# Attention with a learned bias and a top-1 mixture of experts: q and k rows laid out twice by the host

## The chip, the cores and the metric

The kernel runs on one core of a Trainium2 chip. The metric is the device time of an execution in microseconds (us), of which medians are given. The engines are TensorE (PE; its weight loads are listed as PEld), VectorE (DVE), ScalarE (ACT) and GpSimd (POOL); SyncE (SP) issues most of the DMA transfers. SBUF is the on-chip memory of 128 partitions, PSUM the memory that TensorE writes its results to, HBM the device memory.

## The reference

Eight batches, eight heads, 576 tokens, head size 64, all in fp32. A small network of the log-distance of two positions gives a bias for every head, the same for all batches; the output of the attention goes through a top-1 mixture of eight experts.

```python
scores = scale * np.matmul(q, k.transpose(0, 1, 3, 2))       # B, H, S, S
x = (psi_rel / psi_i)[..., None]                             # log distances
bias = np.maximum(x @ w1 + b1, 0.0) @ w2                     # S, S, H
scores = scores + bias.transpose(2, 0, 1)[None]
attn = np.exp(scores - np.max(scores, axis=-1, keepdims=True))
attn = attn / (np.sum(attn, axis=-1, keepdims=True) + 1e-09)
x = np.matmul(attn, v)                                       # then rows of 512
...
ye = np.maximum(x[mask] @ w1[e], 0.0) @ w2[e]                # expert of the largest gate logit
out[mask] = gate_w[mask, None] * ye
```

## The kernel before

**Pairs.** The attention goes by batch and pair of heads: u = 4 b + pr, 32 pairs, each with five query tiles (four of 128 rows and one of 64). A query tile's scores for both heads go to PSUM (L253, two heads of 576 columns in halves of 288), VectorE adds the bias and takes the maximum (`less`, L275), ScalarE takes the exponential with its sum (L283), TensorE transposes (L293, L297), VectorE and ScalarE copy the transposed tiles (L304 to L312), TensorE multiplies by v (L318, L320), ScalarE copies the result (`osb`, L475), and another product with the identity turns it into token rows (`x`, L336), which VectorE scales (L351).

**Split of q and k.** TensorE multiplies in the type fp32r, so each of q and k is split into hi (rounded to fp32r) and lo (the rest). The score product contracts 128 rows: of q, hi in partitions 0 to 63 and lo in 64 to 127 (`qs`); of k, once hi in both halves (`k1`), once lo in both (`k2`). In HBM a pair's q and k lie with the first head in partitions 0 to 63 and the second in 64 to 127. `load_raw` (L211) brings them to `qn` (704 columns: 576, 64 zeros, 64 again) and `kn` (640 columns), one buffer each; `split_hi` (L217) casts on ScalarE for both heads at once; `split_lo` (L222) subtracts in place on VectorE; `move` (L236) then moves rows between partitions, by SP's queue: for q two transfers of hi and two of lo, for k four and four, each of 64 partitions.

**Opening.** The bias is made by 36 groups (`bias_group`): four `h` tiles (the first on ScalarE, L722, three on VectorE, L724; a ring of seven), eight matmuls (L729), one activation to `ob` (L731; a ring of three), and a DMA (L734) that spreads `ob` over 16 partitions eight apart of the bias tile. Pairs 0 and 1 are loaded first; ten query tiles of them (`attend`) are interleaved with the groups, with LEAD = 15 groups ahead of the first tile and RATE = 4 ahead of each that follows; pair 2 is loaded in the eighth step. The order of the instructions here is the scheduler's, by data and buffers.

**Steady pairs.** Pairs 2 to 31 run from a list of words, one string a query tile: `FULL` for pairs 2 to 29, `LAST` for 30 and 31, next to the first expert's weights. SA and SB are the two score halves, T0 to T2 transposes, p products with v, w the rest of those and the `osb` copy, x the token rows, r the routing's ranks. TensorE follows the words; VectorE and ScalarE get their order from a planner that emits whatever is due first by fixed costs. The splits and loads of the next pairs are placed by `AHEAD`, by query tile (hi, lo, load and v, with the pair that is meant and 0 for q, 1 for k). Once a batch the routing of its tokens runs on VectorE and POOL scatters its rows to HBM. After the pairs come the experts.

Of the kernel before, what the change touches and what calls it, by code (L numbers as in the profile page):

```python
# [21 lines left out]
P = 128  # L22
B, H, S, D = 8, 8, 576, 64
SH = S // 2
NPAIR = H // 2
# [7 lines left out]
QW, KW = S + 2 * 64, S + 64  # L33
# [15 lines left out]
AHEAD = [[("lo", 1, 1), ("load", 1, 0)], [("v", 1, 2)], [("load", 2, 1), ("hi", 1, 0)], [("lo", 1, 0)], [("hi", 2, 1)]]  # L49
FULL = ["SA SB T2 T0", "w SA SB T0 p p p p T2 T1 w", "SA T2 T0 SB T1 r", "SA x SB T0 p p p p T2 T1", "SA SB T0 T1 x T2"]  # L50
LAST = ["SA SB T2 T0", "w SA SB T0 p p p p T2 T1 w", "SA x T0 SB T2 T1", "SA x p p T0 SB T2 T1 p p w", "SA T0 SB p p p p w x T2 T1",
# [104 lines left out]
def attention(tc, ctx, q, kt, vm, ltab, bcst, gate, gt, cm, cmat, ival, tail0, pcst, bias, xs, plan, moe):  # L156
# [4 lines left out]
    hp_ = ctx.enter_context(tc.tile_pool(name="hi", bufs=1))  # L161
# [33 lines left out]
    def load_pair(b, pr):  # L195
        u = b * NPAIR + pr
        for x in range(2):
            load_raw(u, x)
            split_hi(u, x)
            split_lo(u, x)  # L200
            move(u, x)
        load_v(u)
# [6 lines left out]
    def load_raw(u, x):  # L209
        t = raw.tile([P, (QW, KW)[x]], F32, name=("qn", "kn")[x])  # L210
        nc.sync.dma_start(out=t, in_=(q, kt)[x][divmod(u, NPAIR)])  # L211
        raws[u, x] = [t]

    def split_hi(u, x):
        src, = raws[u, x]
        hi = hp_.tile([P, QW], F32R, name="hi")[:, :src.shape[-1]]
        nc.scalar.copy(out=hi, in_=src)  # L217
        raws[u, x].append(hi)

    def split_lo(u, x):  # L220
        src, hi = raws[u, x]
        nc.vector.tensor_tensor(out=src.bitcast(F32R), in0=src, in1=hi.bitcast(F32), op=ALU.subtract)  # L222

    def move(u, x):

        src, hi = raws.pop((u, x))
        if x:
            tiles = [kq.tile([P, 2, KW], F32R, name=n) for n in ("k1", "k2")]
            places = [[(t, h) for h in range(2)] for t in tiles]
        else:  # L230
            tiles = [kq.tile([P, 2, QW], F32R, name="qs")]
            places = [[(tiles[0], h)] for h in range(2)]
        for part, to in zip((hi.bitcast(F32), src), places):
            for t, half in to:
                for h in range(2):
                    nc.sync.dma_start(out=t[64 * half:64 * half + 64, h].bitcast(F32), in_=part[64 * h:64 * h + 64])  # L236
        loaded[u, x] = tiles
# [139 lines left out]
    def attend_units(units, words, beside):  # L377
# [139 lines left out]
        def extra(kind, u, x, *deps):  # L517
            if u >= total:
                return
            here = [(last_pe[0], 0), *deps]  # L520
            if kind == "load":
                loads[u, x] = add("any", 0, lambda: load_raw(u, x), *here, *([(subs[u - 1, x], 0.5)] if (u - 1, x) in subs else []))
            elif kind == "v":
                add("any", 0, lambda: load_v(u), *here)
            elif kind == "hi":
                splits[u, x] = add("ACT", 0.65, lambda: split_hi(u, x), *here, *([(loads[u, x], 3.0)] if (u, x) in loads else []),
                                   *([(subs["last"], 3.2)] if "last" in subs else []))
            elif kind == "lo":
                def emit():
                    split_lo(u, x)  # L530
                    move(u, x)
                subs["last"] = subs[u, x] = add("DVE", 0.77, emit, (splits[u, x], 0.8), *here)
                moved.setdefault(u, []).append((subs[u, x], 4.0))

        for k, st in enumerate(steps):
# [18 lines left out]
            beside.at(k, st, steps, add, extra, last_pe[0], ranked)  # L554
# [213 lines left out]
    class Beside:  # L768
# [12 lines left out]
        def at(self, k, st, steps, add, extra, here, ranked):  # L781
            u, qt = st["u"]["b"] * NPAIR + st["u"]["pr"], st["sc"].qt
            j = k - (len(steps) - 10)
            if j < 0:
                if k == 0:
                    extra("hi", u + 1, 1)
                for kind, v, x in AHEAD[qt]:
                    extra(kind, u + v, x)
                if j == -1:
                    extra("load", u + 2, 0)  # L790
                return
            if j == 0:
                extra("lo", u + 1, 1)
                extra("hi", u + 1, 0)
                add("DVE", 1.2, first_expert, (here, 0), (ranked[-1], 0))
            elif j == 1:
                extra("lo", u + 1, 0)
                extra("v", u + 1, 2)
# [264 lines left out]
def layout(inputs):  # L1063
# [7 lines left out]
    q = np.concatenate([q, np.zeros_like(q[..., :64]), q[..., S - 64:]], axis=-1).reshape(B, NPAIR, 2 * D, QW)  # L1071
    k = np.concatenate([k, k[..., :64]], axis=-1).reshape(B, NPAIR, 2 * D, KW)
# [57 lines left out]
```

## Time and profile before

| what | us |
|---|---|
| median of three runs | 1164.29 (1162.99 to 1167.45) |
| the profiled execution, whole | 1165.9 |
| its span in the trace | 1164.0 |
| TensorE busy | 1082.2 (93%) |
| VectorE busy | 666.7 (57%) |
| ScalarE busy | 562.4 (48%) |
| POOL busy | 169.2 (15%) |

The trace is of one execution. Busy time is a mean over stages: the opening up to about 150 us, steady pairs of 17 to 20 us up to about 685 us, then experts. A stage has to be read by itself, in the views of stretches and in the timeline; a DMA share is the mean busy share of 16 DMA engines, and can come out a little over 1, as the records of packets overlap. Of a transfer listed as DMA_DIRECT2D on SP's queue (SPq), the time is that of its issue, not of the transfer.

### The profile page before, as it was taken

Reading aid. Unit: us, or ns where it says so; the run is one execution under the profiler, and the core shown is the slowest. Engines: PE = TensorE matmul, PEld = TensorE weight load, DVE = VectorE, ACT = ScalarE, POOL = GpSimd, SP = SyncE. Lnnn points to the kernel's source line nnn. Section 1 sums busy time; section 2 is a strip of 40 time slices with the busy share of each in tenths; the row PEclk is TensorE's granted clock in tenths of the full one; section 3 lists DMA queues with packets and bytes.
Section 4 is the critical chain, followed back from the end, with each engine's and each line's share of the span. In section 5 each row is a group of like instructions: output and inputs, shape, how many; then the busy total and the mean of one; then the engine's idle time right before and its main releaser. Section 6 shows DMA issues by size and latency. Waiting matters only on the chain. (4 is left out here: it accounts for less than half of the span.)

```text
span 1164.0 us, 20696 instructions
## 1 busy us (share of the span) xinstructions
PE 1082.2 (93%) x7260; PEld 881.3 (76%) x7260; DVE 666.7 (57%) x1746; ACT 562.4 (48%) x1311; POOL 169.2 (15%) x192
## 2 busy tenths in 40 slices
PE   6599899999999999999998989999999899999894
PEld 3256687777777778787786778898888788888783
DVE  6487678787777877878778664422413232414141
ACT  5587576776767767677676631111312111313030
POOL 0000002001020010200102022500041230032320
PEclk9799999999999999999999989999999999999998
DMA  8945676767766668766777416410331600342400
GB/s 221 208 121 121 173 176 181 204 165 203 196 187 183 175 198 191 197 178 173 209 175 207 152 55 237 180 46 28 120 135 64 241 28 19 120 145 73 172 19 28
DMA packets 70084, 171.80 MB, mean 148 GB/s; under 512 B 11298, under 2 KB 11810, under 8 KB 69794
## 3 DMA queue, kind: packets, MB, share of 16 engines
q1 hardware_dynamic: 63682, 150.07, 46.9%
q0 software_dynamic: 5920, 18.95, 4.5%
q8 instruction: 72, 1.18, 0.5%
q14 instruction: 122, 1.00, 0.3%
q10 hardware_dynamic: 288, 0.59, 0.1%
HBM read 75.00 MB, written 23.97 MB: 85 GB/s over the span
## 5 line engine op out<-in xcount | busy, mean ns | idle before, releaser
L253 PE MATMUL s<-k,qs 128*128 128x288 f32 x1280 | 239.9, 319 | 17.1 <-ACT ob L731 7.5
L275 DVE CUSTOM_DVE_ANT_0 t<-s,bias 128x576 f32<-128x576 f32 x288 | 213.5, 753 | 60.4 <-PE s L253 39.7
L283 ACT ACTIVATE a<-t,mn 128x576 f32<-128x576 f32 x288 | 223.6, 777 | 26.3 <-DVE mn L275 20.9
L908 PE MATMUL psh<-bias,bias 128*128 128x384 f32 (+2 forms) x1248 | 206.6, 322 | 12.1 <-issue 8.3
L253 PEld LDWEIGHTS s<-k,qs 128*128 128x128 f32 x1280 | 184.8, 191 | 38.3 <-DVE mn L275 10.7
L908 PEld LDWEIGHTS psh<-bias,bias 128*128 128x128 f32 x1248 | 198.5, 194 | 17.7 <-issue 10.0
L297 PE MATMUL tps<-gt,a 128*128 128x128 f32 x1152 | 171.2, 275 | 6.7 <-ACT at L312 3.6
L898 ACT ACTIVATE bias<-psh 128x384 fp32r<-128x384 f32 (+2 forms) x104 | 46.6, 452 | 259.2 <-PE psh L908 258.8
L297 PEld LDWEIGHTS tps<-gt,a 128*128 128x128 f32 x1152 | 136.3, 141 | 16.8 <-ACT a L283 5.3
L318 PE MATMUL o<-at,v 128*64 128x256 f32 (+4 forms) x1152 | 143.2, 389 | 5.1 <-issue 5.0
L899 DVE SCALAR_TENSOR_TENSOR bias<-psh,bias 128x384 fp32r<-128x384 f32 (+2 forms) x104 | 52.0, 505 | 111.9 <-ACT bias L898 111.7
L318 PEld LDWEIGHTS o<-at,v 128*64 128x64 f32 x1152 | 74.7, 138 | 52.1 <-issue 16.0
L310 DVE COPY at<-tps 128x512 f32<-128x512 f32 x128 | 88.1, 689 | 41.6 <-PE tps L297 39.8
L312 ACT COPY at<-tps 128x512 f32<-128x512 f32 x128 | 74.5, 582 | 74.6 <-PE tps L297 66.7
L940 PE MATMUL psy<-w2h,bias 128*128 128x512 f32 (+1 forms) x224 | 89.5, 401 | 3.3 <-DVE y L944 2.8
L941 PE MATMUL psy<-w2l,bias 128*128 128x512 f32 (+1 forms) x224 | 88.3, 396 | 0.0
L585 POOL TENSOR_TENSOR cs<-cs,oh 128x8 f32<-128x8 f32 x40 | 12.2, 305 | 522.0 <-DVE oh L580 519.5
L942 PE MATMUL psy<-w2h,bias 128*128 128x512 f32 (+1 forms) x224 | 87.3, 397 | 0.0
L945 POOL DMA_INDIRECT out<-y,ids x32 | 31.4, 983 | 276.0 <-DVE y L944 236.4
L729 PE MATMUL s<-h,bc 128*32 128x288 f32 x576 | 55.9, 466 | 14.0 <-ACT ob L731 11.2
L883 ACT CAST bias<-tps 128x384 fp32r<-128x384 f32 (+2 forms) x60 | 24.9, 462 | 86.7 <-PE tps L881 75.4
L724 DVE TENSOR_SCALAR h<-lt,bc,nb1t 128x576 f32<-128x576 f32 x108 | 55.6, 577 | 14.9 <-PE s L729 14.8
(165 smaller groups left out, 1346.7 us busy)
## 6 DMA issues: line engine op xcount, KB each, us to landing
k<-hi SPq DMA_DIRECT2D x128, 160.0 KB
k<-kn SPq DMA_DIRECT2D x128, 160.0 KB
bias<-in_wl SPq DMA_DIRECT2D x28, 512.0 KB
qn<-in_q SPq DMA_DIRECT2D x32, 352.0 KB
qs<-hi SPq DMA_DIRECT2D x64, 176.0 KB
qs<-qn SPq DMA_DIRECT2D x64, 176.0 KB
kn<-in_kt SPq DMA_DIRECT2D x32, 320.0 KB
v<-in_vm SPq DMA_DIRECT2D x32, 320.0 KB
```

What stands on the lines that cost most here:

```text
L253: return nc.tensor.matmul(s[:, hf, :SH], loaded[u, 0][0][:, hh, i:i + P], loaded[u, 1][second][:, hh, k0 + hf * SH:k0 + hf * SH + SH], sta ...
L275: nc.vector.tensor_tensor_reduce(out=self.t[i], in0=self.s[i][:, :, :SH], in1=bt.rearrange("p (a c) -> p a c", a=2), op0=ALU.add, op1=ALU. ...
L283: nc.scalar.activation(out=self.a[:, j * S:(j + 1) * S], in_=self.t[i].rearrange("p a c -> p (a c)"), func=AF.Exp, bias=self.mn[:, i:i + 1 ...
L297: nc.tensor.transpose(tps[:, c], a[:, k0:k0 + P], ident)
L310: nc.vector.tensor_copy(out=at[:, 4:8, c0:c0 + n], in_=tps)
L312: nc.scalar.copy(out=at[:, :4, c0:c0 + n], in_=tps)
L318: mm = nc.tensor.matmul(o[64 * hh:64 * hh + 64, :N], v[:, c, 64 * hh:64 * hh + 64], at[:, 4 * hh + c, :N], start=c == 0, stop=False, skip_ ...
L729: nc.tensor.matmul(ps[32 * j:32 * j + 32, hf, :SH], w2bd, hs[j][:, hf * SH:(hf + 1) * SH], start=True, stop=True)
L908: nc.tensor.matmul(ps[:, :N], w[c][:, k0:k0 + P], x[kc][:, :N], start=i + kc == 0, stop=i == 2 and kc == KC - 1)
L940: nc.tensor.matmul(ps[:n], a, wh, start=f == 0, stop=False)
L941: nc.tensor.matmul(ps[:n], a, wo, start=False, stop=False)
L942: nc.tensor.matmul(ps[:n], b, wh, start=False, stop=f == FC - 1)
```

## The change

The host writes each head's 64 rows of q and of k twice, one copy below the other, so that a head fills all 128 partitions, and sets both heads side by side. A load (`load`, L210 of the kernel after) brings 1408 columns of q or 1280 of k. The cast of a head's hi goes straight into `qs` or `k1` (L217, 128 partitions, one for each head); the subtraction (L221) goes straight into `k2`, or, for q, into the upper 64 partitions of `qs`. Counts over the 32 pairs: casts 64 before and 128 after, subtractions 64 and 128, moves 384 and none, loads of q and k 64 and 64 of twice the size. The tile of hi is dropped; the raw tiles are twice as large, and the ring of `h` has six tiles instead of seven. `AHEAD` is dropped: `FULL` and `LAST` have words for each cast (hq0 to hk1), subtraction (lq0 to lk1), load (dq, dk) and v, and most other words are in new places too. After the eighth step of the opening both tensors of pair 3 are loaded, where it was k alone.

```diff
-FULL = ["SA SB T2 T0", "w SA SB T0 p p p p T2 T1 w", "SA T2 T0 SB T1 r", "SA x SB T0 p p p p T2 T1", "SA SB T0 T1 x T2"]
+FULL = ["SA SB x hq0 T2 T0", "SA SB hk0 hk1 T0 p p p p T2 T1 lk0", "w r hq1 lk1 dk SA T2 SB T0 T1 x", "SA lq0 T0 SB T2 lq1 p p p dq p T1", "SA T0 SB w v T1 T2"]
...
-    hp_ = ctx.enter_context(tc.tile_pool(name="hi", bufs=1))
...
-    def load_raw(u, x):
-        t = raw.tile([P, (QW, KW)[x]], F32, name=("qn", "kn")[x])
+    def load(u, x):
+        t = raw.tile([P, 2, (QW, KW)[x]], F32, name=("qn", "kn")[x])
         nc.sync.dma_start(out=t, in_=(q, kt)[x][divmod(u, NPAIR)])
...
-        hi = hp_.tile([P, QW], F32R, name="hi")[:, :src.shape[-1]]
-        nc.scalar.copy(out=hi, in_=src)
...
-        nc.vector.tensor_tensor(out=src.bitcast(F32R), in0=src, in1=hi.bitcast(F32), op=ALU.subtract)
...
-        for part, to in zip((hi.bitcast(F32), src), places):
-            for t, half in to:
-                for h in range(2):
-                    nc.sync.dma_start(out=t[64 * half:64 * half + 64, h].bitcast(F32), in_=part[64 * h:64 * h + 64])
...
+    def split_hi(u, x, h):
+
+        if (u, x) not in loaded:
+            loaded[u, x] = [kq.tile([P, 2, KW], F32R, name=n) for n in ("k1", "k2")] if x else [kq.tile([P, 2, QW], F32R, name="qs")]
+        nc.scalar.copy(out=loaded[u, x][0][:, h], in_=raws[u, x][:, h])
+
+    def split_lo(u, x, h):
+        at = slice(0 if x else 64, P)
+        nc.vector.tensor_tensor(out=loaded[u, x][-1][at, h], in0=raws[u, x][at, h], in1=loaded[u, x][0][at, h].bitcast(F32), op=ALU.subtract)
...
-        hp = es.enter_context(tc.tile_pool(name="hp", bufs=7))
+        hp = es.enter_context(tc.tile_pool(name="hp", bufs=6))
...
-                load_raw(3, 1)
+                load(3, 1)
+                load(3, 0)
...
-    q = np.concatenate([q, np.zeros_like(q[..., :64]), q[..., S - 64:]], axis=-1).reshape(B, NPAIR, 2 * D, QW)
-    k = np.concatenate([k, k[..., :64]], axis=-1).reshape(B, NPAIR, 2 * D, KW)
+    q = np.concatenate([q, np.zeros_like(q[..., :64]), q[..., S - 64:]], axis=-1)
+    k = np.concatenate([k, k[..., :64]], axis=-1)
+    q, k = (np.concatenate([a, a], axis=-2).swapaxes(2, 3) for a in (q, k))
```

SP's queue in the opening, before, from the moves of pair 0's k (`k1` gets hi, `k2` lo) to those of pair 1's q; `bias0` is the first query tile's bias:

```order
L236 DMA k1_193<-hi_190 64x640 x4
L236 DMA k2_194<-kn_188 64x640 x4
L211 DMA qn_205<-in_q 128x704
L734 DMA bias0_67<-ob_332 16x8x576
L211 DMA kn_215<-in_kt 128x640
L734 DMA bias0_67<-ob_352 16x8x576
L734 DMA bias0_67<-ob_372 16x8x576
L236 DMA qs_210<-hi_207 64x704 x2
L236 DMA qs_210<-qn_205 64x704 x2
```

The same place after, from the second bias transfer to the k load of pair 2:

```order
L718 DMA bias0_67<-ob_249 16x8x576
L210 DMA qn_192<-in_q 128x1408
L718 DMA bias0_67<-ob_269 16x8x576
L210 DMA kn_199<-in_kt 128x1280
L718 DMA bias0_67<-ob_289 16x8x576
L718 DMA bias0_67<-ob_309 16x8x576
L210 DMA qn_1357<-in_q 128x1408
L718 DMA bias0_67<-ob_329 16x8x576
L210 DMA kn_1364<-in_kt 128x1280
```

The moves are gone from the row, and the loads of pairs 1 and 2 stand among the first seven bias transfers.

ScalarE in the fifth steady pair, before, about the `osb` copy of the last three query tiles (`at` is the transposed attention, `a` its exponential):

```order
L283 ACTIVATE a_2747,r_2702<-t_2745,mn_2738 128x576
L306 COPY at_2741<-tps_2754 128x128
L475 COPY osb_2773<-o_2735 128x320
L306 COPY at_2741<-tps_2775 128x128
L312 COPY at_2741<-tps_2777 128x4x128
L283 ACTIVATE a_2800,r_2799<-t_2784,mn_2783 128x576
L217 CAST hi_2812<-qn_2695 128x704
L283 ACTIVATE a_2800,r_2799<-t_2802,mn_2783 128x576
```

After, the same copy:

```order
L267 ACTIVATE a_2660,r_2617<-t_2649,mn_2641 128x576
L290 COPY at_2653<-tps_2665 128x128
L217 CAST k1_2674<-kn_2525 128x640 x2
L459 COPY osb_2694<-o_2644 128x320
L290 COPY at_2653<-tps_2687 128x128
L217 CAST qs_2647<-qn_2560 128x704
L296 COPY at_2653<-tps_2697 128x4x128
L267 ACTIVATE a_2719,r_2718<-t_2703,mn_2702 128x576
L267 ACTIVATE a_2719,r_2718<-t_2712,mn_2702 128x576
```

Both k casts of the next pair now stand right ahead of that copy, and a q cast two rows behind it.

VectorE in the same pair, before, from the scores of the second query tile on (ISA on L275 is `less`: `t` is the sum, `mn` the maximum):

```order
L275 ISA t_2555,mn_2554<-s_2539,bias2_69 128x576
L275 ISA mn_2554 128x1
L275 ISA t_2573,mn_2554<-s_2557,bias2_69 128x576
L275 ISA mn_2554 128x1
L310 COPY at_2512<-tps_2563 128x4x128
L275 ISA t_2593,mn_2592<-s_2575,bias3_70 128x576
L275 ISA mn_2592 128x1
...
L222 TENSOR_TENSOR qn_2466<-qn_2466,hi_2583 128x704
```

After, the same query tiles:

```order
L221 TENSOR_TENSOR k2_2675<-kn_2525,k1_2674 128x640
L259 ISA t_2703,mn_2702<-s_2680,bias2_69 128x576
L259 ISA mn_2702 128x1
L259 ISA t_2712,mn_2702<-s_2689,bias2_69 128x576
L259 ISA mn_2702 128x1
L294 COPY at_2653<-tps_2706 128x4x128
L221 TENSOR_TENSOR k2_2675<-kn_2525,k1_2674 128x640
L259 ISA t_2740,mn_2739<-s_2722,bias3_70 128x576
L259 ISA mn_2739 128x1
L221 TENSOR_TENSOR qs_2647<-qn_2560,qs_2647 64x704
L259 ISA t_2759,mn_2739<-s_2734,bias3_70 128x576
L259 ISA mn_2739 128x1
```

Where one subtraction stood there are now three of the pair's four (the fourth follows at once), one between each two of the maxima.

## Rows read from the trace of the kernel before

**Rows 1.** Stretches: length, busy PE, PEld, DVE, ACT, POOL, PEclk, DMA share, GB/s

```profile
5.00:10.00 5.00, 4.14 (x43) 2.51 (x46) 4.45 (x12) 3.42 (x6) 0.00 (x0) 1.00 0.96 362
20.00:23.00 3.00, 1.06 (x16) 0.42 (x16) 0.95 (x2) 1.85 (x3) 0.00 (x0) 0.99 1.08 216
45.00:53.00 8.00, 1.42 (x14) 0.63 (x12) 3.31 (x6) 3.05 (x4) 0.00 (x0) 0.83 1.04 216
53.00:103.00 50.00, 49.12 (x501) 27.16 (x502) 40.87 (x100) 40.50 (x73) 0.00 (x0) 0.96 0.46 119
```

**Rows 2.** Timeline of the opening: start us, length, engine, work, [idle before it]

```profile
5.20 2.54 DVE L724 TENSOR_SCALAR h<-lt,bc,nb1t 128x576 f32<-128x576 f32 x5
...
12.09 4.50 DVE L724 TENSOR_SCALAR h<-lt,bc,nb1t 128x576 f32<-128x576 f32 x9
...
51.96 0.74 ACT L731 ACTIVATE ob<-s,cb 128x576 f32<-128x576 f32 x1 [2.40 <-DMA bias<-ob]
...
52.75 1.33 PE L253 MATMUL s<-k,qs 128*128 128x288 f32 x4 [6.58 <-ACT ob L731]
```

**Rows 3.** DMA issues: operands, queue, count, size of one transfer

```profile
k<-hi SPq DMA_DIRECT2D x128, 160.0 KB
...
qn<-in_q SPq DMA_DIRECT2D x32, 352.0 KB
...
qs<-hi SPq DMA_DIRECT2D x64, 176.0 KB
...
kn<-in_kt SPq DMA_DIRECT2D x32, 320.0 KB
...
v<-in_vm SPq DMA_DIRECT2D x32, 320.0 KB
...
bias<-ob SPq DMA_DIRECT2D x32, 288.0 KB
```

**Rows 4.** By line and shape: count | busy us, mean ns | idle before

```profile
L729 PE MATMUL s<-h,bc 128*32 128x288 f32 x576 | 55.9, 466 | 14.0 <-ACT ob L731 11.2 <-DVE h L724 1.9 <-ACT h L722 0.9
...
L724 DVE TENSOR_SCALAR h<-lt,bc,nb1t 128x576 f32<-128x576 f32 x108 | 55.6, 577 | 14.9 <-PE s L729 14.8
...
L722 ACT ACTIVATE h<-lt,bc 128x576 f32<-128x576 f32 x36 | 31.0, 867 | 10.5 <-PE s L729 8.5 <-DVE bc L705 2.0
...
L222 DVE TENSOR_TENSOR qn<-qn,hi 128x704 fp32r<-128x704 f32 x32 | 28.4, 888 | 6.5 <-ACT hi L217 6.5
...
L731 ACT ACTIVATE ob<-s,cb 128x576 f32<-128x576 f32 x36 | 26.3, 729 | 9.3 <-DMA bias<-ob 7.2 <-PE s L729 1.8 <-ACT osb L373 0.3
...
L222 DVE TENSOR_TENSOR kn<-kn,hi 128x640 fp32r<-128x640 f32 x32 | 26.2, 819 | 1.9 <-ACT hi L217 1.8
...
L217 ACT CAST hi<-qn 128x704 fp32r<-128x704 f32 x32 | 24.7, 772 | 7.2 <-DMA bias<-ob 3.9 <-DMA k<-hi 3.3
...
L217 ACT CAST hi<-kn 128x640 fp32r<-128x640 f32 x32 | 23.1, 720 | 2.3 <-DMA qs<-hi 2.2
```

**Rows 5.** Timeline of TensorE at two successive steps with bias groups

```profile
64.05 0.79 PE L253 MATMUL s<-k,qs 128*128 128x288 f32 x4
...
73.96 0.81 PE L253 MATMUL s<-k,qs 128*128 128x288 f32 x4
```

**Rows 6.** Timeline of TensorE where pairs 1 and 2 start

```profile
121.86 0.49 PE L253 MATMUL s<-k,qs 128*128 128x288 f32 x1 [2.10 <-issue]
...
144.75 1.65 PE L253 MATMUL s<-k,qs 128*128 128x288 f32 x8 [1.88 <-DMA qs<-qn]
```

**Rows 7.** Stretches of two steady pairs

```profile
367.90:384.95 17.05, 17.05 (x130) 13.74 (x128) 13.24 (x37) 12.69 (x33) 0.00 (x0) 1.00 0.71 181
384.95:402.45 17.50, 17.20 (x130) 13.75 (x128) 14.60 (x42) 12.60 (x33) 1.00 (x2) 1.00 0.58 156
```

**Rows 8.** Timeline of ScalarE in the pair of the stretch from 367.90

```profile
368.70 0.43 ACT L475 COPY osb<-o 128x320 f32<-128x320 f32 x1 [0.71 <-PE o L320]
```

**Rows 9.** Timeline at a place that comes once a batch

```profile
347.14 2.37 PE L318 MATMUL o<-at,v 128*64 128x320 f32 x16 [1.32 <-issue]
```

More of the change, by code (lines that the diff above doesn't have):

```diff
@@ L197, in load_pair @@
         for x in range(2):
[L198 to L201, printed above, removed]
+            load(u, x)
+            for h in range(2):
+                split_hi(u, x, h)
+                split_lo(u, x, h)
         load_v(u)
@@ L207, in load_v @@
         loaded[u, 2] = v
-    def load_raw(u, x):
-        t = raw.tile([P, (QW, KW)[x]], F32, name=("qn", "kn")[x])
+    def load(u, x):
+        t = raw.tile([P, 2, (QW, KW)[x]], F32, name=("qn", "kn")[x])
         nc.sync.dma_start(out=t, in_=(q, kt)[x][divmod(u, NPAIR)])
-        raws[u, x] = [t]
-    def split_hi(u, x):
-        src, = raws[u, x]
-        hi = hp_.tile([P, QW], F32R, name="hi")[:, :src.shape[-1]]
-        nc.scalar.copy(out=hi, in_=src)
-        raws[u, x].append(hi)
-    def split_lo(u, x):
-        src, hi = raws[u, x]
-        nc.vector.tensor_tensor(out=src.bitcast(F32R), in0=src, in1=hi.bitcast(F32), op=ALU.subtract)
[L224 to L232, printed above, removed]
-        for part, to in zip((hi.bitcast(F32), src), places):
-            for t, half in to:
-                for h in range(2):
-                    nc.sync.dma_start(out=t[64 * half:64 * half + 64, h].bitcast(F32), in_=part[64 * h:64 * h + 64])
-        loaded[u, x] = tiles
+        raws[u, x] = t
+    def split_hi(u, x, h):
[5 more added lines that the diff above has]
+        nc.vector.tensor_tensor(out=loaded[u, x][-1][at, h], in0=raws[u, x][at, h], in1=loaded[u, x][0][at, h].bitcast(F32), op=ALU.subtract)
     xsb = {}
@@ L515, in attend_units, with extra @@
         splits, loads, subs = {}, {}, {}
-        def extra(kind, u, x, *deps):
+        def extra(kind, u, x, h=None):
             if u >= total:
                 return
-            here = [(last_pe[0], 0), *deps]
+            here = [(last_pe[0], 0)] if last_pe[0] else []
             if kind == "load":
-                loads[u, x] = add("any", 0, lambda: load_raw(u, x), *here, *([(subs[u - 1, x], 0.5)] if (u - 1, x) in subs else []))
+                loads[u, x] = add("any", 0, lambda: load(u, x), *here, *subs.get((u - 1, x), []))
             elif kind == "v":
@@ L525, in extra @@
             elif kind == "hi":
-                splits[u, x] = add("ACT", 0.65, lambda: split_hi(u, x), *here, *([(loads[u, x], 3.0)] if (u, x) in loads else []),
-                                   *([(subs["last"], 3.2)] if "last" in subs else []))
+                splits[u, x, h] = add("ACT", 0.65, lambda: split_hi(u, x, h), *here, *([(loads[u, x], 5.0)] if (u, x) in loads else []))
             elif kind == "lo":
[L529 to L533, printed above, removed]
+                op = add("DVE", 0.77, lambda: split_lo(u, x, h), (splits[u, x, h], 0.8), *here)
+                moved.setdefault(u, []).append((op, 0.95))
+                subs.setdefault((u, x), []).append((op, 0.9))
         for k, st in enumerate(steps):
@@ L553, in attend_units @@
                     st["all"] = True
-            beside.at(k, st, steps, add, extra, last_pe[0], ranked)
+                elif word in EXTRAS:
+                    kind, ahead, *which = EXTRAS[word]
+                    extra(kind, st["u"]["b"] * NPAIR + st["u"]["pr"] + ahead, *which)
+            beside.at(k, st, steps, add, last_pe[0], ranked)
         assert not turned and not ended
@@ L779, in chunk, with at @@
             next(self.g, None)
-        def at(self, k, st, steps, add, extra, here, ranked):
-            u, qt = st["u"]["b"] * NPAIR + st["u"]["pr"], st["sc"].qt
+        def at(self, k, st, steps, add, here, ranked):
             j = k - (len(steps) - 10)
[L784 to L791, printed above, removed]
             if j == 0:
-                extra("lo", u + 1, 1)
-                extra("hi", u + 1, 0)
                 add("DVE", 1.2, first_expert, (here, 0), (ranked[-1], 0))
-            elif j == 1:
-                extra("lo", u + 1, 0)
-                extra("v", u + 1, 2)
             elif j == 4:
```

4 lines of the change are left out of this document (2 added, 2 removed).

## The prediction, made before the kernel ran

> **What bounds the kernel now.** I read the stretches of the opening first, then its timeline, then the mean times of the operations that the change touches, and last the stretches of two steady pairs.
>
> From 5 to 10 us the queues carry loads from HBM: 362 GB/s at a DMA share of 0.96 [rows 1]. From 20 to 23 us they carry almost only moves between partitions: the share is 1.08, but the rate 216 GB/s. From 45 to 53 us, with moves, bias tiles and a load together, it is 1.04 and again 216, while TensorE is busy 1.42 of 8 us and VectorE 3.31. From 53 to 103 us, when two pairs' moves are over, the share is 0.46 at 119 GB/s and TensorE is busy 49.12 of 50 us. So the time up to the first scores hangs on the DMA engines, and what follows on TensorE. The timeline shows the joint: the first scores start at 52.75 us after 6.58 us without work, released by `ob` (the activation that empties a bias group's PSUM), and that activation, at 51.96, had waited 2.40 us for a bias DMA to give back one of three `ob` tiles [rows 2].
>
> In the steady pairs TensorE is the bound: a pair takes 17.05 us with TensorE busy 17.05; VectorE has 13.24 and ScalarE 12.69 of it. The next pair has VectorE 14.60 of 17.50, since a batch's routing falls there [rows 7]. Taking DMA traffic from such a pair is worth nothing directly; filling VectorE or ScalarE costs only where a result that TensorE waits for comes later.
>
> **Opening, up to the first score.** By the sizes of one transfer [rows 3] a pair's twelve moves are 4 x 176 + 8 x 160 = 1984 KB and its q and k loads 352 + 320 = 672 KB. After, the moves are gone and the loads are 1344 KB. At the measured rates [rows 1] a pair goes from 2.03 MB / 216 = 9.4 us plus 0.69 MB / 362 = 1.9 us to 1.38 MB / 362 = 3.8 us: 7.5 us less, 15 us for the two pairs ahead of the first score. What DMA must still do from 5 us on: three pairs' q and k (4.13 MB / 362 = 11.4 us), two of `v` (0.66 / 362 = 1.8 us) and fifteen bias tiles of 288 KB [rows 3]. These run at 119 GB/s at share 0.46 [rows 1], so 259 at full share: 4.42 MB / 259 = 17.1 us. It ends at 5 + 30.3 = 35.3 us and is no longer last.
>
> Next late is VectorE. Ahead of the first score stand fifteen groups with three `h` each on VectorE, now with eight subtractions. Lower bound: nine `h` in a row took 4.50 us [rows 2], so 45 x 0.50 = 22.5; the subtractions 4 x 0.888 + 4 x 0.819 = 6.8 [rows 4]; from 5.20, with 1.5 for the last matmuls and `ob`: 36.0. Upper bound: 45 x 0.577 = 26.0 by the mean, 6.8, and the ring of `h` tiles, which shrinks from seven to six. A group takes four, so the next group's third and fourth wait for the second half of this group's matmuls: two `h` and two matmuls, 2 x 0.577 + 2 x 0.466 = 2.1 against 3 x 0.577 = 1.73 of work, 0.35 a group, 15 x 0.35 = 5.3. That ends at 5.2 + 26.0 + 6.8 + 5.3 + 1.5 = 44.8. ScalarE has 15 x (0.867 + 0.729) + 4 x 0.772 + 4 x 0.720 = 29.9 us and lies inside. One wait is added: the second pair's q load may start only when the first pair's subtractions have read the one raw tile, and SP's bias DMAs stand behind it; `ob`, and with it ScalarE, would back up. It costs nothing while subtractions are done as soon as casts are, and is in the upper bound otherwise. I take the middle, 40.5: **-12.2 us** (-17 to -8).
>
> One rule speaks against this size. Moves run at 216 GB/s and loads at 362 [rows 1]; the sum goes by these. The Trainium skill, "DMA: Bandwidth & Descriptors", section "Where 436 GB/s comes from", has the opposite order: HBM to SBUF bound near 358, SBUF to SBUF by the fabric's 435. By it two pairs' traffic would fall by 2 x (2.03 / 0.435 - 0.69 / 0.358) = 5.5 us, an estimate, for -12.2. The trace agrees on loads and contradicts it on these moves of 64 partitions.
>
> **The five steps that follow** (four bias groups and a query tile each) start 9.91 us apart [rows 5] and are TensorE's. The smaller `h` ring can open gaps here: none, or 0.35 x 20 x a half = 3.5. The first step took 11.30 (52.75 to 64.05) with the granted clock at 0.96 over the stretch [rows 1] after the idle opening; that may come back if TensorE is busier before. **+0.3** (-1.4 to +3.5).
>
> **First pairs' starts.** TensorE idles 2.10 us at 121.86 and 1.88 at 144.75, the second for a q move [rows 6]. Both moves go; two casts and two subtractions of q and k take their place closely ahead of the scores. Gain 4.0 at most; loss, one cast plus one subtraction late, 1.6 less what hides it: **-3** (-4 to +1).
>
> **Steady pairs**, 28 of them. Added on ScalarE 0.772 + 0.720 = 1.49 us a pair; on VectorE 0.888 + 0.819 = 1.71, or 0.82 if the q subtraction, now on half of the partitions for each head, took half the time [rows 4]. I take 1.71, as both shapes have the same columns. Busy would be 14.18 and 14.95 of 17.05, and VectorE 16.31 of 17.50 in the routing pair [rows 7]. That fits; what decides is the place. Both k casts now stand directly ahead of the `osb` copy (the sums for the output) on ScalarE, 1.44 us; before, nothing of the kind did, and `osb` waited 0.71 us there for its matmuls [rows 8], so 0.73 at most lies on its path, and its reader on TensorE, the product with the identity, comes later. On VectorE four subtractions stand between the score maxima, one at a time. SP's queue loses twelve moves a pair, and its loads wait for the subtractions of the pair ahead, with most of a pair's time to land. **0** (0 to +14, half a microsecond for each pair).
>
> **The stall once a batch.** At 347.14 TensorE had been idle for 1.32 us for no reason that the profile shows [rows 9]; the batch's scatters and a pair's k moves are in the queues then. Seven batches' ends can hold one, 7 x 1.32 = 9.2. If the moves cause it, it goes; if the scatters do, it stays, or the doubled loads prolong it by half. The rows don't tell: **0** (-9 to +4).
>
> **Last two pairs and experts.** Loads and casts double there too, TensorE's work is unchanged: **0** (-1 to +2).
>
> Sum: -12.2 + 0.3 - 3 = -14.9. The profiled execution took 1165.9 us (span 1164.0), 1.6 above the median of 1164.29; 1165.9 - 14.9 = 1151.0, and against the median 1149.4, given as **1149.5**.
>
> **Rivals.**
> A, the sum: 1149.5, own range 1143 to 1157. For: DMA shares over 1 with TensorE idle. Against: thin cover for the casts.
> B, the batch stalls go too: 1149.5 - 9.2 = 1140.3. For: k moves are in the queues at the stall. Against: the scatters stay.
> C, the six `h` tiles, the eight subtractions and the load that waits for them hold each other up, a subtraction standing between `h` and its matmul: first score near 47.5, so 1149.5 + 7 = 1156.5 (1154 to 1162). For: VectorE's upper bound is at 44.8 already. Against: the row of nine `h` without a gap.
> D, the other side: the two casts ahead of `osb`, or the subtractions among the score maxima, make TensorE wait in every steady pair. One operation ahead too many is about 0.75 us: 28 x 0.75 = +21, so 1170.5. It decides from 14.9 / 28 = 0.53 us a pair. For: VectorE at 88 to 93% of a pair. Against: 2.1 us of slack in VectorE, 2.9 in ScalarE.
> E, the doubled load lands late at the q cast: 0.72 MB / 181 (the pair's rate [rows 7]) is 4 us, and 0.4 us a pair makes +11: 1160.5. Against: the queue is free of twelve moves.
> F, a move's byte costs no more than a load's, the 216 being the bias tiles' doing: DMA gives 2 x (2.03 - 0.69) / 0.362 = 7.4 us, so 1164.3 - 7.4 + 0.3 - 3 = 1154.2. Against: 20 to 23 us holds hardly a bias tile. The page named above goes this way.
>
> **How the numbers follow.** A 0.62, B 0.12, C 0.11, D 0.08, E 0.04, F 0.03. Half a per cent, 5.8 us, is about what a measurement of this kernel can tell from no change; its bounds are 1158.5 and 1170.1. A, B and F are faster, C half faster and half same, E same; D is slower by 0.05 and same by 0.03. Faster 0.62 + 0.12 + 0.03 + 0.05 = 0.82, same 0.06 + 0.03 + 0.04 = 0.13, slower 0.05. The range goes from below B, 1137, to 1163, past C and E; D's upper half is left out.
>
> **What would show it.** In the changed kernel's profile: no transfer from SBUF to `qs` or `k`; a DMA share below 1 between 10 and 40 us; the first score at 36 to 45 us (47 or later is C); steps still 9.9 us apart; no gaps at 121.86 and 144.75 less the gain; a pair at 17.05 with TensorE busy throughout (17.6 or more is D, with `osb` or the score maxima as what TensorE waited for; with a q load named it is E); 128 casts of some 0.75 us. It would be wrong if doubled loads ran at the moves' rate, or if steady pairs gained or lost 0.5 us each, since 28 of them weigh as much as the opening.

## The result and the profile after

The changed kernel takes 1122.12 us (median of four runs, 1116.94 to 1123.67) where the kernel before takes 1163.64: a ratio of 0.963, 95% interval 0.959 to 0.967. The forecast was 1149.5 with a range of 1137 to 1163; the gain is 41.5 us and not 14.9. The profiled execution has a span of 1120.7 us against 1164.0, so the two traces differ by 43.3 us, and I account for those.

The stretches of the kernel after, first of the opening, then of three steady pairs: plain, with a batch's routing, with the scatters of a batch. Columns as in [rows 1].

```profile
5.00:10.00 5.00, 4.30 (x41) 2.30 (x44) 3.63 (x10) 3.32 (x6) 0.00 (x0) 1.00 1.02 415
10.00:20.00 10.00, 6.59 (x55) 1.94 (x50) 8.76 (x15) 8.57 (x13) 0.00 (x0) 1.00 0.83 250
30.00:40.00 10.00, 8.79 (x91) 3.07 (x80) 7.99 (x16) 7.66 (x11) 0.00 (x0) 1.00 0.59 154
54.00:95.00 41.00, 39.90 (x404) 22.21 (x403) 34.43 (x84) 32.76 (x60) 0.00 (x0) 1.00 0.44 114
352.70:369.50 16.80, 16.80 (x130) 13.76 (x128) 15.04 (x39) 13.82 (x35) 0.00 (x0) 1.00 0.28 93
369.50:387.10 17.60, 17.57 (x134) 14.30 (x133) 16.42 (x51) 13.94 (x35) 1.11 (x6) 1.00 0.32 99
387.10:404.20 17.10, 17.06 (x130) 13.75 (x129) 15.60 (x43) 14.06 (x36) 6.08 (x6) 1.00 0.50 165
```

The same three sorts of pair before, the first two lines about the pairs of [rows 7], with bounds that are the starts of the pairs' first scores:

```profile
378.00:395.10 17.10, 17.10 (x129) 13.77 (x129) 13.25 (x36) 12.73 (x34) 0.00 (x0) 1.00 0.68 180
395.10:413.60 18.50, 17.88 (x133) 14.22 (x133) 16.27 (x52) 13.05 (x35) 2.88 (x8) 1.00 0.62 166
413.60:432.80 19.20, 17.46 (x129) 13.82 (x129) 13.21 (x36) 12.75 (x35) 3.84 (x5) 1.00 0.74 223
```

Two things stand out. The DMA share fell everywhere, as forecast. And every sort of pair got shorter although VectorE and ScalarE have more to do in it, which was not forecast: VectorE is busy 15.04 of 16.80 us and the pair is 0.2 us shorter; by the medians over all such pairs (table below) the routing pair lost 0.9 us and the scatter pair 1.9.

The timeline of TensorE after, first scores of the first two steps and the start of pairs 2 and 3 (where [rows 5] and [rows 6] answer; pairs count from 0, so the heading of [rows 6], which says 1 and 2, names them one too low):

```profile
43.94 0.79 PE L237 MATMUL s<-k,qs 128*128 128x288 f32 x4
...
54.25 0.80 PE L237 MATMUL s<-k,qs 128*128 128x288 f32 x4
64.61 0.80 PE L237 MATMUL s<-k,qs 128*128 128x288 f32 x4
...
110.59 1.67 PE L237 MATMUL s<-k,qs 128*128 128x288 f32 x8
130.34 1.30 PE L237 MATMUL s<-k,qs 128*128 128x288 f32 x8
```

From such starts in both traces the gain adds up like this:

| up to | before | after | gained so far | in this part |
|---|---|---|---|---|
| first score | 52.75 | 43.94 | 8.8 | 8.8 |
| sixth query tile | 103.68 | 95.67 | 8.0 | -0.8 |
| pair 4 | 163.30 | 147.17 | 16.1 | 8.1 |
| pair 30 | 629.48 | 592.41 | 37.1 | 21.0 |
| third query tile of pair 31 | 653.81 | 613.06 | 40.8 | 3.7 |
| end | 1164.0 | 1120.7 | 43.3 | 2.5 |

(The query tiles of pairs 30 and 31 are interleaved, so the row before the last covers the first five query tiles of the two.) The last 2.5 us (the rest of the two pairs and the experts, whose program hardly changed) are no effect: in the twelve other traces of this study the same part takes 505 to 517 us. Half of the gain is in the 26 pairs from 4 to 29, for which I had put 0. These pairs as one stretch, before and after:

```profile
163.30:629.48 466.18, 452.09 (x3332) 361.68 (x3332) 365.49 (x1049) 332.12 (x841) 43.37 (x79) 1.00 0.70 187
147.17:592.41 445.24, 443.86 (x3334) 361.60 (x3331) 401.95 (x1097) 360.59 (x891) 42.80 (x77) 1.00 0.37 117
```

TensorE's idle time fell from 14.1 to 1.4 us, and the time for which it is shown as busy with the same matmuls from 452.1 to 443.9.

In the opening after, the idle time of VectorE that the smaller ring of `h` was to give can be read off. Timeline of VectorE, [idle before <- what ended it]:

```profile
39.80 1.56 DVE L708 TENSOR_SCALAR h<-lt,bc,nb1t 128x576 f32<-128x576 f32 x3 [0.37 <-PE s L713]
41.73 1.56 DVE L708 TENSOR_SCALAR h<-lt,bc,nb1t 128x576 f32<-128x576 f32 x3 [0.36 <-PE s L713]
```

A group takes 1.93 us: 1.56 of `h` and 0.37 of waiting for TensorE to give a tile back. The casts and subtractions after, by line and shape, where [rows 4] answers:

```profile
L221 DVE TENSOR_TENSOR qs<-qn,qs 64x704 fp32r<-64x704 f32 x64 | 56.7, 889 | 3.0 <-ACT qs L217 1.1
L708 DVE TENSOR_SCALAR h<-lt,bc,nb1t 128x576 f32<-128x576 f32 x108 | 56.1, 575 | 13.9 <-PE s L713 11.9 <-ACT ob L715 1.8
L221 DVE TENSOR_TENSOR k<-kn,k 128x640 fp32r<-128x640 f32 x64 | 51.9, 814 | 2.5 <-ACT k L217 2.5
L217 ACT CAST qs<-qn 128x704 fp32r<-128x704 f32 x64 | 49.7, 781 | 2.9 <-DMA qn<-in_q 2.9
L217 ACT CAST k<-kn 128x640 fp32r<-128x640 f32 x64 | 43.5, 727 | 2.7 <-DMA kn<-in_kt 2.2 <-PE s L237 0.5
```

There are twice as many, each as long as before; the q subtraction on 64 partitions takes 889 ns where on 128 it took 888.

### The profile page after: what moved, and what is told of

It reads as the page before. It is cut to its first block, busy times and chain, and to the rows that moved or that the text cites. A ratio compares the mean times of both kernels' runs of the same rounds, so it can differ in the third digit from the quotient of the medians.

```text
span 1120.7 us, 20113 instructions
## 1 busy us (share of the span) xinstructions
PE 1069.4 (95%) x7260; PEld 876.4 (78%) x7260; DVE 710.5 (63%) x1810; ACT 597.2 (53%) x1375; POOL 171.3 (15%) x192
## 5 line engine op out<-in xcount | busy, mean ns | idle before, releaser
L237 PE MATMUL s<-k,qs 128*128 128x288 f32 x1280 | 237.0, 316 | 4.8 <-DVE mn L259 2.2
L259 DVE CUSTOM_DVE_ANT_0 t<-s,bias 128x576 f32<-128x576 f32 x288 | 210.6, 753 | 19.8 <-ACT a L267 5.4
L237 PEld LDWEIGHTS s<-k,qs 128*128 128x128 f32 x1280 | 181.3, 189 | 20.4 <-DVE mn L259 4.5
L281 PEld LDWEIGHTS tps<-gt,a 128*128 128x128 f32 x1152 | 134.4, 141 | 24.4 <-issue 10.5
L569 POOL TENSOR_TENSOR cs<-cs,oh 128x8 f32<-128x8 f32 x40 | 8.1, 201 | 427.5 <-DVE oh L564 425.0
L713 PE MATMUL s<-h,bc 128*32 128x288 f32 x576 | 59.4, 432 | 9.5 <-DVE h L708 7.3
L915 DVE TENSOR_SCALAR y<-psy,g 128x512 f32<-128x512 f32 (+1 forms) x32 | 23.8, 747 | 67.8 <-PE psy L913 67.8
```

What stands on the lines that cost most here:

```text
L237: return nc.tensor.matmul(s[:, hf, :SH], loaded[u, 0][0][:, hh, i:i + P], loaded[u, 1][second][:, hh, k0 + hf * SH:k0 + hf * SH + SH], sta ...
L259: nc.vector.tensor_tensor_reduce(out=self.t[i], in0=self.s[i][:, :, :SH], in1=bt.rearrange("p (a c) -> p a c", a=2), op0=ALU.add, op1=ALU. ...
L281: nc.tensor.transpose(tps[:, c], a[:, k0:k0 + P], ident)
L713: nc.tensor.matmul(ps[32 * j:32 * j + 32, hf, :SH], w2bd, hs[j][:, hf * SH:(hf + 1) * SH], start=True, stop=True)
```

## The experiments

The change has two halves that the diff makes at once: the data path (rows twice, no moves, operations by head) and the order (new words for TensorE's work, new places for casts, subtractions and loads). The theories after the result: **M**, the moves' traffic is what the steady pairs had lost; **O**, the new order gained there. In the tables a plain pair is one of the two of each batch without routing or scatters; the numbers are medians over pairs 4 to 29 of the time from a pair's first score to the next pair's, from the trace. The runs with one head, with new words or new places alone on the new data path, with the operations in a row, with transfers from the fourth pair on and with six `h` tiles were executed once each; their pair times rest on the many pairs of one trace, their whole times on one execution.

**The data path alone, in the old order.** The changed loads, casts and subtractions, six `h` tiles, but with the old words and the old places:

```diff
+    def split_hi(u, x):          # both heads, called where the old one was
+        loaded[u, x] = [kq.tile([P, 2, KW], F32R, name=n) for n in ("k1", "k2")] if x else [kq.tile([P, 2, QW], F32R, name="qs")]
+        for h in range(2):
+            nc.scalar.copy(out=loaded[u, x][0][:, h], in_=raws[u, x][:, h])
```

> The changed data path (rows laid out twice by the host, no moves, doubled casts and subtractions, six h tiles) in the order of before: the old words and the old places of casts, subtractions and loads. Theory M: the moves' DMA traffic is what before lost, in the opening and in the steady pairs too; then the order matters little, a pair after the batch's scatters takes about 17.1 us and not 19.0, and the whole is 1120 to 1130. Theory O: the steady pairs gained by the new order; then the first score is at 43 to 44 us as after the change, but the steady pairs stay at 17.05, 17.05, 18.5 and 19.0 us as before, and the whole is 1140 to 1150.

Measured: 1148.06 us (1144.90 to 1149.17), ratio 0.985 (0.978 to 0.992). The forecast of 1149.5 is near what this kernel takes: the sum was about right for the data path and left out the order. That is in part luck, as two of its terms are off in opposite ways: this trace gains 7.1 us up to the first score where 12.2 were forecast, and 7.5 in the first pairs where 3 were. Its first score is at 45.68, and its pairs are no better than before:

```profile
365.50:382.70 17.20, 17.06 (x128) 13.63 (x127) 14.82 (x38) 13.66 (x36) 0.00 (x0) 1.00 0.29 92
382.70:401.80 19.10, 18.30 (x133) 14.18 (x133) 17.65 (x54) 14.10 (x36) 3.10 (x8) 1.00 0.30 104
401.80:420.40 18.60, 17.69 (x129) 13.79 (x129) 14.72 (x38) 13.70 (x36) 4.46 (x5) 1.00 0.45 147
```

The DMA share is down to 0.29 as after the change, VectorE has the added work, and the pair takes 17.26 us, the routing pair 19.07. M falls for the steady pairs, as far as the doubled work does not hide a gain; the next run parts the two.

**One head's operations only.** To part the moves' absence from the doubled work, the same kernel with `range(1)` for the heads:

> The run with the old order and no moves, with casts and subtractions of the first head alone (both heads' scores use the first head's q and k, so the output of every second head is left wrong): as many operations as before, each as long, and no moves. It shows what the moves' absence alone is worth in a steady pair. Theory M (moves cost steady pairs something, above all beside the scatters): plain pairs 16.9 to 17.05, routing 18.4, pairs with scatters 17.1 to 17.9 where before had 19.0. Theory N (moves cost a steady pair nothing, the stall belongs to the scatters): 17.05, 18.5, 18.6 to 19.0. Either way, the difference to the run with both heads' operations, 17.26, 19.06 and 17.9 to 18.6, is what doubling them costs in the old places.

Measured: 17.06, 18.49 and 18.57 us, the first two to 0.01 us those of before. So the moves cost plain and routing pairs nothing, as the forecast had it, and a scatter pair some 0.5 us (before's sum over pairs 4 to 29 is known to some 6 us only: 466.2 here, 472.3 in the run with six `h` tiles below, which has the same steady program; without moves it repeats to 2); doubling casts and subtractions in the old places costs 0.2 us in a plain and 0.6 in a routing pair.

**The two halves of the order.** First the new words for TensorE with the old places, then the old words with the new places:

```diff
-FULL = ["SA SB x hq0 T2 T0", "SA SB hk0 hk1 T0 p p p p T2 T1 lk0", "w r hq1 lk1 dk SA T2 SB T0 T1 x", "SA lq0 T0 SB T2 lq1 p p p dq p T1", "SA T0 SB w v T1 T2"]
+FULL = ["SA SB hq0 T2 T0", "w SA SB hk0 hk1 T0 p p p p T2 T1 w lk0", "hq1 lk1 dk SA T2 T0 SB T1 r", "SA lq0 x SB T0 lq1 p p p dq p T2 T1", "SA SB v T0 T1 x T2"]
```

> The changed data path with the new places of TensorE's work, but with casts, subtractions and loads where before had them (both heads' casts in a row, both subtractions in a row). Theory W: pairs 16.85, routing pairs 17.6, whole 1120 to 1130. Theory P (what gains is that casts and subtractions are spread one by one over the pair): pairs 17.26, routing pairs 19.0 as in the run with the old order, whole 1140 to 1150.

> The other half: the changed data path with the old places of TensorE's work, casts, subtractions and loads spread as the changed kernel has them. Theory W: pairs 17.2, routing pairs 18.5 to 19, whole 1140 to 1150. Theory P: pairs 16.85 to 16.95, whole 1120 to 1130.

Measured: 1169.63 us with the new words alone, over before and over what either theory had; 1128.10 with the new places alone, as P had it, with plain pairs a little over P's 16.95. The four combinations on the new data path, with before and the one-head run beside them:

| kernel | TensorE's words | places of casts, subtractions, loads | plain | routing | scatters | pairs 4 to 29 |
|---|---|---|---|---|---|---|
| before | old | old | 17.06 | 18.49 | 19.05 | 466.2 |
| one head's operations, no moves | old | old | 17.06 | 18.49 | 18.57 | 462.7 |
| data path alone | old | old | 17.26 | 19.07 | 18.58 | 468.2 |
| new words | new | old | 18.36 | 18.59 | 18.31 | 478.7 |
| new places | old | new | 17.04 | 17.88 | 17.04 | 449.2 |
| changed kernel | new | new | 16.85 | 17.59 | 17.15 | 445.2 |

The new places are worth 19.0 us, the new words 4.0 on top of them, and without the new places the new words cost 10.5. In the new-words run the row of a plain pair, and TensorE's waits in it (total, times, longest), show a wait of the kind that rival D had put, an operation too many ahead of a result that TensorE needs:

```profile
371.20:389.60 18.40, 17.38 (x130) 13.87 (x128) 16.09 (x45) 13.98 (x35) 0.00 (x0) 1.00 0.25 77
```

```profile
PE o L303 <- DVE at L293: 0.8, 1, 0.8
PE s L238 <- DVE mn L260: 0.2, 1, 0.2
```

The longer wait in the timeline (the line numbers are this run's):

```profile
372.90 0.60 PE L282 MATMUL tps<-gt,a 128*128 128x128 f32 x4
...
374.25 1.55 DVE L219 TENSOR_TENSOR k<-kn,k 128x640 fp32r<-128x640 f32 x2
...
375.72 0.68 DVE L293 COPY at<-tps 128x512 f32<-128x512 f32 x1
...
376.46 1.84 PE L303 MATMUL o<-at,v 128*64 128x320 f32 x12 [0.82 <-DVE at L293]
```

The transposes are done at 373.50, but VectorE's copy of them stands behind both k subtractions (1.55 us) and starts at 375.72; TensorE's product with v waits for that copy, which D had not named; the shorter wait is for a score maximum, as D had it. The work is the same as after the change; its place differs, and one thing with the place. In the three runs with old places on the new data path the planner works with its fixed costs of before, 0.65 us for a cast and 0.77 for a subtraction of a tensor; where both heads are cast and subtracted, as here, it thus counts one operation where two are emitted. How much of what the old places cost is due to that count was not tried apart.

**Is it the spreading?** The changed kernel with the two heads' operations directly behind one another:

```diff
-FULL = ["SA SB x hq0 T2 T0", "SA SB hk0 hk1 T0 p p p p T2 T1 lk0", "w r hq1 lk1 dk SA T2 SB T0 T1 x", "SA lq0 T0 SB T2 lq1 p p p dq p T1", ...]
+FULL = ["SA SB x hq0 hq1 T2 T0", "SA SB hk0 hk1 T0 p p p p T2 T1 lk0 lk1", "w r dk SA T2 SB T0 T1 x", "SA lq0 lq1 T0 SB T2 p p p dq p T1", ...]
```

> The changed kernel with the operations of one tensor in a row again: hq0 hq1, lk0 lk1 and lq0 lq1 one directly behind the other, each pair at the place that its first has in the changed kernel (hk0 hk1 stand together in both). Theory S (the gain comes of the spreading, since a single operation of 0.75 us fits into VectorE's and ScalarE's slack and two do not): pairs at 17.3 or more, whole 1135 to 1150. Theory L (it comes of the places as such, wherever in the pair both stand): pairs 16.85 to 17.0, whole 1120 to 1130.

Measured: 1136.74 us, inside the bounds of S, but not in the way that S had it. Plain pairs take 16.85, as after the change, except the one of each batch behind the scatter pair, which takes 18.75; routing pairs take 17.95 (17.59). The stretch of such a pair shows VectorE and ScalarE with time to spare:

```profile
338.40:357.20 18.80, 17.43 (x130) 13.84 (x129) 14.94 (x42) 13.99 (x34) 5.05 (x6) 1.00 0.46 156
```

Its timeline shows ScalarE standing still for 1.9 us from 344.98 and VectorE for 1.5 from 345.40, released together:

```profile
346.86 0.27 ACT L288 COPY at<-tps 128x128 f32<-128x128 f32 x1 [1.88 <-PE s L235]
346.92 0.69 DVE L292 COPY at<-tps 128x512 f32<-128x512 f32 x1 [1.52 <-PE s L235]
```

The halt resembles the one at [rows 9], again about the last scatter, which runs from 344.70 to 345.61; it is there in each of the six batches. The changed kernel has no place in these pairs where both engines stand still for 0.7 us together. Over pairs 4 to 29 this run takes 458.9 us, 19.8 less than the new words with the old places and 13.7 more than the changed kernel. So most of the gain is in the places and stays with two operations in a row. Of the 13.7 us that spreading adds, 11.9 are in the pairs behind the scatters, 2 us a batch, with the halt in them, and 0.4 us a batch are in the routing pairs. What halts the engines stays open: it is not the moves alone (it is there without them), and a kernel without the scatters was not tried.

**Do the new words do without the change?** The kernel before, with moves, single operations and old places, and the new words:

> The kernel before with the changed kernel's places for scores, transposes, products, token rows and ranks on TensorE (FULL and LAST without the words of casts, subtractions and loads), its own casts, subtractions, moves and loads where they were. Theory W (the steady gain lies in these places, and needs nothing of the new data path): steady pairs 16.85, routing pairs 17.6, whole 1135 to 1148. Theory X (the gain needs the moves gone, since the later products and their copies meet the moves or the old casts): pairs at 17.0 or more, routing pairs 18.5, whole 1158 to 1175.

Measured: 1169.83 us (median of ten executions: nine from 1162.47 to 1174.34, and one of 2645.86 that the ratio leaves out), ratio 1.006 (1.003 to 1.009): slower by 0.6%. Routing pairs gain (17.66), plain ones lose (18.01), though three of the six behind the scatters take 16.8. The whole and the plain pairs are as X had them, the routing pairs as W had them. X's reason, that the gain needs the moves gone, is not shown: the new-words run above has no moves and loses too. What the new words do not go with is the old places.

**Do the new places do with moves?** The changed kernel with 8 transfers of 64 partitions added to each pair, behind its subtractions; once for all pairs, once from the fourth on:

```diff
+        if u > 2:                                   # True for all pairs
+            for t in [raws[u, x], *(loaded[u, x] if x else [])]:
+                nc.sync.dma_start(out=t[64:, h], in_=t[:64, h])
```

> The changed kernel, in its own order, with 8 transfers of 64 partitions added to every pair by SP's queue (upper half of the raw tiles, of k1 and of k2 written with the lower half, which holds the same), 1312 KB a pair where before had 1984. Theory M: the first score goes back to 48 to 53 us, pairs after the scatters to 18 to 19 us, the whole to 1145 to 1160. Theory O: first score as under M, but the steady pairs stay near 16.85, and the whole is 1128 to 1135.

> The same transfers, but only from the fourth pair on: the opening is as after the change. Theory M: first score at 43 to 44 us, pairs after the scatters 18 to 19 us, the whole 8 to 10 us under the run with all of them, 1137 to 1150. Theory O: within 5 us of the changed kernel, 1118 to 1127.

Measured: 1246.46 and 1222.59 us, far over both theories: plain pairs of 20.2 and 20.5 us instead of 16.85. Waits in the second run, first of SP's queue over two pairs, then of ScalarE and of TensorE in one of them, a scatter pair:

```profile
SPq L210 <- DMA qn<-qn: 6.4, 2, 4.7
```

```profile
ACT qs L217 <- DMA qn<-in_q: 3.1, 1, 3.1
```

```profile
PE tps L284 <- ACT at L299: 2.0, 1, 2.0
PE tps L284 <- DVE at L297: 0.7, 1, 0.7
```

The raw tile is read by the transfers until late, the next load into it starts late, the q cast waits 3.1 us for it at its new place, and ScalarE's copies and exponentials stand behind that cast. This is rival E, with the added transfers as its cause. So the new places do not go with transfers that hold the raw tile. From this I take it that the moves had forced the casts of before into their early places, so that loads and moves land in time, and that this freedom, and not the traffic, is what the absence of moves is worth in the steady pairs. It is an argument and not shown: the added transfers also write the raw tile, which the moves of before did not, and before's own moves in an order that leaves loads more time were not tried. In the opening, with the transfers back, the first score is at 52.51 and the DMA share from 10 to 52 us at 0.96 to 1.03; the raw tiles are held longer there too, so the traffic is not alone.

**The ring of `h`.** The kernel before with `bufs=6` for `h`, and the changed kernel with `bufs=8`, for which the opening has one tile of transposed attention instead of two:

> The kernel before with six h tiles instead of seven. If the ring is what made the steps with bias groups longer after the change (10.35 us where before had 9.91), they are 10.3 to 10.4 here too, and the whole is 1 to 3 us over before; if it is the doubled loads or the casts, they stay at 9.9. The first score is DMA's and stays at 52 to 54 us.

> The changed kernel with eight h tiles, for which the opening's tiles of transposed attention go from two to one. If the ring of six holds VectorE 0.37 us in every bias group, that idle time goes: the first score comes at 40 to 41 us instead of 43.7, steps with bias groups at 9.9 us or less instead of 10.35, and the whole is 4 to 6 us under the changed kernel, less what the one tile costs in the last query tiles of the opening (up to 2). If the ring is not the cause, first score and steps stay.

Measured: before with six tiles has its steps 10.35 us apart (9.91 with seven), first score at 52.39, 1172.26 us; the whole is further over before than expected, as pairs 4 to 29, with the same program, took 6.1 us longer in this execution. The changed kernel with eight has steps 9.11 us apart on average and its first score at 41.70, a miss of the 40 to 41; 1116.58 us, ratio 0.962 (0.957 to 0.966). For the steps the ring is the cause in both. That it moves the first score is not shown, since 41.70 lies within what the six-tile kernels have (below). The row of the eight-tile run over the five steps is to be read beside [rows 1]:

```profile
41.80:87.30 45.50, 44.17 (x502) 26.09 (x502) 40.91 (x102) 40.52 (x75) 0.00 (x0) 1.00 0.50 133
```

TensorE did 502 matmuls here in 45.5 us; in the kernel before it did 501 of the same work in 50 us, and was shown as busy 49.12 of them [rows 1]. Much of that difference is the clock: over the first step of before, 11.30 us long, the granted clock was 0.81. The four steps behind it have a granted clock of 1.00 in both, first before, then with eight tiles:

```profile
64.05:103.68 39.63, 38.75 (x406) 21.48 (x404) 34.32 (x85) 33.03 (x60) 0.00 (x0) 1.00 0.47 120
50.81:87.24 36.43, 35.94 (x406) 21.44 (x404) 32.99 (x83) 32.27 (x62) 0.00 (x0) 1.00 0.50 132
```

The same 406 matmuls were shown as busy for 38.75 us and then for 35.94: a busy share of 0.98 was no floor.

**Is the version with eight tiles faster?** Both on one chip, five rounds:

> The changed kernel unaltered, on the same chip as the next run, for a comparison of the two: 1118 to 1124, first score 42 to 45 us, steps 10.35 us.

> Eight h tiles and one tile of transposed attention in the opening, again. By the earlier trace the third pair starts 5.5 us sooner and the rest is alike: 3 to 6 us under the run beside it. If what the opening gains is lost in the last query tiles or behind, the two are within 2 us.

Measured: 1122.81 us (ratio 0.9645, 0.961 to 0.968) and 1122.48 (0.9636, 0.960 to 0.967): no difference that can be told. The steps gain 6.2 us in the trace, the first score comes 1.4 later and the single tile gives 2.0 us back in the last query tiles (pair 2 starts at 104.75 against 107.48 beside it); the rest is within what executions differ by. The changed kernel's first score alone was at 40.77 to 45.68 us in the seven traces with its opening, 42.9 on average; this run's 40.77 is under the 42 to 45 expected.

## Why the prediction was wrong, point by point

**Steady pairs: the step that failed.** I put 0 (0 to +14) for them, having read that "TensorE is the bound: a pair takes 17.05 us with TensorE busy 17.05". The gain there is 21.0 us: 12.7 are idle time of TensorE that went, 8.2 are busy time. Three mistakes are in that one step. A busy time of TensorE was taken for a floor; the same 130 matmuls took 16.80 after. Only a plain pair was read closely: [rows 7] shows it and most of the routing pair, but the routing pair's 18.5 us and the scatter pair's 19.0, with TensorE idle 0.6 and 1.7 us in them, were not put down as something that an order could win. By the rows above, before's pairs 4 to 29 hold 466.2 - 26 x 16.85 = 28 us over the plain pair of after; the change took 21 of them. And the new order was weighed only as a risk: I asked whether the new places fit, not what the old ones cost. The durations in the step were right: VectorE 14.95 forecast and 15.04 measured in a plain pair, ScalarE 14.18 and 13.82. That VectorE's 16.31 and 16.42 in a routing pair agree is luck, since [rows 7] cuts that pair elsewhere; from its first score to the next pair's, before had 16.27 already. For the old places the forecast of no gain holds to 2 us (466.2 and 468.2).

**Opening: right in mechanism, term too large.** 12.2 us were forecast (8 to 17), 8.8 measured, 7.1 to 12.0 in the traces with that opening. DMA's share fell to 0.83 and 0.59, and VectorE is late next, as put. The ring's term was 0.35 us a group and is 0.37. In this trace the score came at 43.94, near the upper bound of 44.8; the mean of the seven traces, 42.9, lies between it and the middle that I took, and with eight tiles the score came no earlier than theirs, so which part of the sum was too small is not shown. The rule on rates of the Trainium skill, "DMA: Bandwidth & Descriptors", section "Where 436 GB/s comes from", would have given -5.5 here, and the gain was larger; its 358 for HBM to SBUF was passed too, with 415 GB/s from 5 to 10 us. With 1312 KB a pair back, the first score moved by 8.6 us, or by 6.8 to 11.7 against the seven traces: two pairs' 2.69 MB at 230 to 395 GB/s, too wide to tell the rate of moves from that of loads in [rows 1]. The Trainium skill, "SBUF — State Buffer", section "Door 1: The DMA port swizzle", says that the top bit of the partition number picks one half of the ports; by it 64 partitions reach half of 435, 218 GB/s as an estimate, and the 216 GB/s of [rows 1] fits that, though no run here varied the partitions.

**Five steps.** +0.3 forecast, +0.8 measured: four steps 0.44 longer, the first 1.0 shorter (10.31 after 11.30), with a granted clock of 1.00 over it where before had 0.81. Both were named.

**First pairs.** -3 forecast, -8.1 measured up to pair 4. The two idle rows of [rows 6] were all that I counted. The one-head run has the whole of it (101.9 us from first score to pair 4, 110.6 before, 103.2 after), so it comes with the data path without moves. 3.3 us are ahead of pair 2's start, with the 2.10 idle before it; 3.1 are in pair 2 and 1.7 in pair 3. These two pairs, before and after:

```profile
121.86:144.75 22.89, 20.34 (x166) 16.77 (x167) 14.06 (x37) 13.93 (x36) 0.00 (x0) 0.93 0.67 179
144.75:163.30 18.55, 18.55 (x127) 15.27 (x128) 12.31 (x29) 11.86 (x31) 0.00 (x0) 0.91 0.66 165
110.59:130.34 19.75, 18.80 (x173) 15.62 (x171) 16.33 (x48) 15.35 (x42) 0.00 (x0) 1.00 0.36 121
130.34:147.17 16.83, 16.83 (x131) 13.79 (x129) 14.84 (x39) 13.85 (x35) 0.00 (x0) 1.00 0.30 97
```

Behind each of the two idle rows the granted clock was down: 0.52 from 121.86 to 125.40 and 0.62 from 144.75 to 149.30, so mostly at the lower of its two levels (1.2 and 2.4 GHz). After, it is 1.00 throughout. Pair 3 shows the price: TensorE is busy all of its 18.55 us, 1.5 more than in the plain pairs that follow at 1.00. So the waits cost their own length and the slower clock behind them; the sum had the first alone, though it named the clock for the opening.

**Last two pairs.** 0 forecast, -3.7 measured for their first five query tiles: 24.34 us before, 20.65 after; in the old order without moves 20.75 with one head's operations and 21.89 with both heads'. So most of it comes with the moves' absence again.

**The batch stall.** 0 forecast, with -9.2 as rival B. In the scatter pairs the change gained 1.9 us each, 11 in the six from pair 4 to 29, but not by B's mechanism: without moves 18.57 remain, with the new places 17.04.

**The rivals' places.** D's kind of wait shows up with the new words and the old places, E's where transfers are added; the changed kernel has neither in its plain pairs. No rival had the order as a gain.

## What to carry to other kernels

A share of 98 or 100% in TensorE's busy column is no floor: the same matmuls were shown as busy for 38.75 us in one run and 35.94 in another. Compare the time of the same matmuls in two stretches, at the same granted clock, before calling them the bound. When a change removes a slow step, ask what that step may have forced, how early its inputs had to be and which queue places they took, and cost the freedom as well as the step. In a loop with several sorts of passes, sum what each sort holds over the shortest one; that sum is what a better order can win.

## What the runs showed of the hardware

From 5 to 10 us, with loads of q and k rows of 5.1 to 5.6 KB in each partition among others, the queues moved 415 GB/s at a DMA share of 1.02; before, with rows half as long, it was 362 at 0.96 [rows 1]. A subtraction on 64 partitions takes as long as on 128 (889 and 888 ns). And about the last scatter of a batch the engines can stand still together with no cause that the profile shows: TensorE for 1.3 us at [rows 9], ScalarE and VectorE for 1.9 and 1.5 us in the run with the operations in a row, where the pair behind the scatters is 1.9 us longer than other plain pairs. Whether it happens depends on the order: the changed kernel has no such halt of ScalarE and VectorE.
